# Sparse attention into a four-expert layer: weights asked for at other steps, a third buffer of v, first sums of x on VectorE, first attention steps in another order

## The chip, the cores and the metric

The kernel runs on one core of a Trainium2 chip. A core has TensorE (PE in the profile; its weight loads are shown apart as PEld), VectorE (DVE), ScalarE (ACT), GpSimd (POOL) and SyncE (SP), which here only issues transfers. The metric is device time in microseconds (us) for one execution, the median of several. The kernel before takes 1242.9 us (three executions: 1242.7, 1242.9 and 1249.59 us).

## What is computed

Attention for 4 batches, 8 heads, 768 positions and 64 channels a head. A query sees the first 8 keys and the 96 latest ones up to its own position, with a bias that falls with distance. Its result, reshaped to 3072 rows of 512, goes through four experts, each two matrix products with a relu between, mixed by given weights:

```python
scores = scale * q @ k.T + bias            # bias = -slope[head] * distance
scores = where(is_global | is_local, scores, -1e9)
x = softmax(scores) @ v                    # then reshaped to (3072, 512)
p = domain_probs / domain_probs.sum(-1)
out = sum over e of p[:, e] * (relu(x @ w1[e]) @ w2[e])
```

Everything is float32. w1 is (4, 512, 1024), w2 is (4, 1024, 512).

## The kernel before

**Batches and units.** The four batches of 768 rows go one after the other. A batch has 16 units (expert, quarter of its 1024 columns). `first(i)` is unit i's product with w1 and the relu, `second(i)` its product with w2, added to the output rows. The order is first(0), first(1), second(0), first(2), second(1) and so on. first yields 5 to 7 times (once for each of its products, which are Strassen-like combinations of blocks of x and of w1), second 6 times (once for each tile of 128 rows). Each yield is a step.

**Two halves of every number.** The big products multiply a rounded high half and a low half of each factor, so each product is three matmuls. x blocks and weights are therefore split first: `high` copies into the rounded type, `low` subtracts it from the source. Tiles w1s and w2s hold split weights, xB and xT split blocks of x and of sums of blocks (T1 to T4). A product of first is six matmuls of 128x384, and the second of these already needs a low half of the weights.

**Weights in batch 0.** `load_w1(i, wait, lead, hold, high)` works in steps: it waits `wait` steps, asks for the raw weights (one transfer into the only buffer raw1), waits `lead` steps, has GpSimd make four sums in `sums` (S1 to S4), waits `hold` steps, and then splits in four slices, a step each: high by ScalarE (for units 0 and 1 by GpSimd), low by GpSimd. `load_w2` does the same without sums. One such generator for unit i+2 starts with each first(i) and each second(i). w1s and w2s have two buffers each. After use they are written out to tiles named kept; batches 1 to 3 fetch them from there, so GpSimd splits weights in batch 0 alone.

**Attention.** Batches 1 to 3 have their attention woven into the units of the batch before (`attention`). Batch 0's attention has nothing to hide under and runs first, in `first_attention`: 12 steps d, each two tiles of 128 queries of one pair of heads, three steps a pair, pairs in the order 0, 2, 1, 3. `start` loads q and k of a pair, `start_v` its v (tiles first_v and first_vg, each with natv = 2 buffers), `turn_qk` transposes two tiles of q and k into early_q and early_k, `scores` multiplies them, `softmax` adds the bias nbias on VectorE and takes the exponential on ScalarE (pb), `turn` transposes the result (pT), `recip` inverts the sums (zr), `weigh_two` multiplies with v, `finish` writes x. Between the steps `forms_of` splits those blocks of x that are finished, and the first weights are loaded.

**What sets the order.** Every engine executes its own instructions in order, SyncE its transfers too: one that waits holds back those behind it. In the first attention and the first 7 steps of the units the order is that of the code (`Ordered.on`); after that a scheduler orders the work of each engine. Operations of these engines go through a helper and carry its line, L42, so instructions are told apart by the tiles they write and read.

## Time and profile before

| | |
|---|---|
| median of three executions | 1242.9 us |
| the profiled execution | 1247.98 us |
| its span, first to last instruction | 1245.7 us |
| PE busy in the span | 1191.1 us (96%) |
| DVE, ACT, POOL busy | 66%, 38%, 16% |
| mean granted TensorE clock | 0.976 of full speed |

Times in the views are microseconds from the start of the span, so the profiled execution's own time has 2.3 us around the span. In an instruction row stand the start, how long it (or the row of merged ones) lasted, engine, line, operation, the tile written and those read, shapes, and the count; in brackets the idle time of that engine just before, and what ended it. In a stretch row stand the busy time of each engine with its number of instructions, then PEclk, the granted TensorE clock (1.00 is 2.4 GHz, 0.50 is 1.2 GHz), the busy share of the transfer engines and GB/s. A wait row says who waited for whom: total us, how many times, the longest.

### The profile page before, as it was taken

What the parts mean: (1) busy time and instruction counts of PE and PEld (TensorE: products, weight loads), DVE (VectorE), ACT (ScalarE), POOL (GpSimd) and SP (SyncE); (2) the same over time, 40 slices, a digit from 0 to 9 for tenths busy, and PEclk for the clock granted to TensorE, in tenths of its full rate; (3) what the DMA queues carried; (4) which work ended last, traced back from release to release, by engine and by line L of the source; (5) the groups of instructions that cost most, each with busy time, mean ns of one, the idle gap of its engine ahead of it and who ended that gap; (6) DMA issues with size and microseconds to landing.
All of it is one profiled execution on the core that took longest, in us unless ns stands there. A gap on an engine that the chain in (4) does not pass through costs nothing.

```text
span 1245.7 us, 18214 instructions
## 1 busy us (share of the span) xinstructions
PE 1191.1 (96%) x6740; PEld 1063.7 (85%) x6740; DVE 826.2 (66%) x1771; ACT 478.1 (38%) x1234; POOL 202.3 (16%) x212
## 2 busy tenths in 40 slices
PE   7689798999999999999999999999999999999998
PEld 6578687878887898999898899989988899999997
DVE  6587455664757675766676877667666776666665
ACT  4444445554663254444443244444434221111110
POOL 3463533536365000000000100000000100000000
PEclk9789898998999999999999999999999999999999
DMA  7547659686598976766665775768474555555532
GB/s 127 113 168 204 203 160 304 194 265 209 178 329 304 276 224 203 227 191 224 210 194 188 249 227 191 213 188 251 154 230 159 201 212 186 188 189 186 186 131 87
DMA packets 146257, 252.97 MB, mean 203 GB/s; under 512 B 108273, under 2 KB 116465, under 8 KB 129777
## 3 DMA queue, kind: packets, MB, share of 16 engines
q1 hardware_dynamic: 142560, 245.44, 62.3%
q10 hardware_dynamic: 3600, 6.29, 1.4%
q8 instruction: 55, 0.90, 0.3%
q14 instruction: 42, 0.34, 0.1%
HBM read 180.41 MB, written 52.43 MB: 187 GB/s over the span
## 4 chain that ended last, share of the span: by engine, by line
PE 84%; POOL 4%; DVE 4%; DMA 3%; ACT 3%; issue 2%; SPq 0%; DVEq 0%; POOLq 0%; ACTq 0%
PE pm L42 73%; PE pt L42 6%; PE ps L42 4%; POOL w1s L42 2%; POOL sums L42 1%; DMA kept<-w1s 1%; POOL w2s L42 1%; DMA k<-in_k_dram 1%; ACT pb L42 1%; DMA qd<-st_q 1%; DMA raw<-in_moe_w_dram 0%; DVE pm L42 0%; DVE h L42 0%; DVE acc L42 0%; ACT xT L42 0%
## 5 line engine op out<-in xcount | busy, mean ns | idle before, releaser
L42 PE MATMUL pm<-w2s,h 128*128 128x512 f32 x2304 | 551.7, 394 | 3.6 <-DVE h L42 3.6
L42 PEld LDWEIGHTS pm<-w2s,h 128*128 128x128 f32 x2304 | 427.6, 188 | 92.9 <-DVE h L42 5.4
L42 DVE SCALAR_TENSOR_TENSOR acc<-pm,prob,acc 128x512 f32<-128x512 f32 x360 | 268.3, 749 | 158.2 <-PE pm L42 156.4
L42 PE MATMUL pm<-xT,w1s 128*128 128x384 f32 x1536 | 308.7, 347 | 6.6 <-POOL w1s L42 4.0
L42 PEld LDWEIGHTS pm<-xT,w1s 128*128 128x128 f32 x1536 | 276.9, 195 | 11.6 <-POOL w1s L42 6.5
L42 PE MATMUL pm<-xB,w1s 128*128 128x384 f32 x1152 | 231.2, 341 | 15.0 <-POOL w1s L42 13.9
L42 PEld LDWEIGHTS pm<-xB,w1s 128*128 128x128 f32 x1152 | 201.9, 189 | 20.9 <-POOL w1s L42 15.2
L42 ACT ACTIVATE h<-pm 128x384 fp32r<-128x384 f32 x256 | 124.8, 491 | 174.7 <-DVE pm L42 172.2
L42 DVE SCALAR_TENSOR_TENSOR h<-pm,h 128x384 fp32r<-128x384 f32 x256 | 140.8, 552 | 17.7 <-ACT h L42 13.0
L42 ACT ACTIVATE pb<-pb,nmax 128x256 f32<-128x256 f32 (+1 forms) x192 | 92.8, 485 | 100.6 <-DVE nmax L42 99.8
L42 ACT COPY p<-pm 128x384 f32<-128x384 f32 x64 | 30.5, 477 | 193.6 <-PE pm L42 184.3
L42 POOL TENSOR_TENSOR xT<-x,xT 128x768 fp32r<-128x768 f32 x3 | 5.5, 1837 | 569.1 <-ACT xT L42 569.1
L42 DVE TENSOR_TENSOR u<-pm,p 128x384 f32<-128x384 f32 x64 | 35.6, 557 | 84.4 <-PE pm L42 64.6
L42 ACT ACTIVATE pb<-pb,zsum 128x256 f32<-128x256 f32 (+1 forms) x144 | 63.3, 484 | 30.3 <-DVE zsum L42 30.2
L42 DVE TENSOR_TENSOR pm<-pm,vv 128x384 f32<-128x384 f32 x128 | 71.5, 559 | 2.0 <-PE pm L42 1.8
L42 POOL TENSOR_TENSOR w2s<-raw,w2s 128x512 fp32r<-128x512 f32 x32 | 42.0, 1333 | 160.1 <-ACT w2s L42 143.6
L42 DVE CUSTOM_DVE_ANT_0 pb<-ps,nbias 128x256 f32<-128x256 f32 (+1 forms) x144 | 52.5, 396 | 12.9 <-PE pt L42 11.1
L42 ACT COPY pT<-pt 128x512 f32<-128x512 f32 (+1 forms) x72 | 39.5, 550 | 55.0 <-PE pt L42 54.8
L42 PE MATMUL pt<-ident,pb 128*128 128x128 f32 x352 | 55.6, 282 | 0.0
L42 DVE TENSOR_TENSOR u<-pm,u 128x384 f32<-128x384 f32 x64 | 35.6, 557 | 28.1 <-PE pm L42 27.6
L42 DVE TENSOR_TENSOR vv<-pm,u 128x384 f32<-128x384 f32 x63 | 35.1, 557 | 27.2 <-PE pm L42 26.7
L42 PEld LDWEIGHTS pt<-ident,pb 128*128 128x128 f32 x352 | 43.2, 145 | 7.3 <-issue 4.5
(102 smaller groups left out, 905.0 us busy)
## 6 DMA issues: line engine op xcount, KB each, us to landing
w1s<-kept SPq DMA_DIRECT2D x48, 1792.0 KB, 7.5
w2s<-kept SPq DMA_DIRECT2D x48, 1024.0 KB, 4.9
kept<-w1s SPq DMA_DIRECT2D x16, 1792.0 KB, 8.6
qd<-st_q SPq DMA_DIRECT2D x96, 192.0 KB, 3.9
raw<-in_moe_w_dram SPq DMA_DIRECT2D x32, 512.0 KB, 6.0
kept<-w2s SPq DMA_DIRECT2D x16, 1024.0 KB, 8.4
out_dram<-acc ACTq DMA_DIRECT2D x24, 256.0 KB, 3.6
q<-in_q_dram SPq DMA_DIRECT2D x24, 192.0 KB, 6.5
```

The lines of the kernel that those rows point to most:

```text
L42: ins = fn(*args, **kwargs)
```

## The change

Six edits; none changes what is computed.

- The pool natv has three buffers of first_v and of first_vg. v of the later pairs is asked for one step after q and k of the same pair.
- In first_attention step 0 is written out ahead of the loop: its softmax comes before the scores of step 1, and the two early tiles of k of step 0 are copied from PSUM by ScalarE.
- w1 of unit 0 is asked for one step sooner, ahead of the second pair's v; w1 of unit 1 one step sooner; w2 of unit 0 eight steps later.
- T1 of the first block of x is subtracted by VectorE instead of GpSimd, and T3 is made at d = 8 and not at d = 9.
- w1 of unit 2 is asked for after 1 step instead of 6, ahead of w2 of unit 1, and split 5 steps sooner; w2 of unit 1 waits 6 steps instead of 12 before its split.
- For every later unit of batch 0, w1 is asked for after 4 steps instead of 9.

```diff
-            ve.tensor_copy(kT[:, ts[0] : ts[1] + 1, :P], tp[:, 2 * P :].rearrange("p (t c) -> p t c", c=P))
+            (ac.copy if d == 0 else ve.tensor_copy)(
+                kT[:, ts[0] : ts[1] + 1, :P], tp[:, 2 * P :].rearrange("p (t c) -> p t c", c=P)
+            )
...
-        start_v(ORDER[0])
         turn_qk(0)
         scores(0)
+        start_v(ORDER[0])
+        start(ORDER[1], slice(0, NQT))
+        softmax(steps[0])
+        next(bias)
         turn_qk(1)
-        yield
-        start(ORDER[1], slice(0, NQT))
+        scores(1)
+        softmax(steps[1])
+        turn_qk(2)
+        yield
         start_v(ORDER[1])
-        for d in range(last + 3):
+        for d in range(1, last + 3):
...
             if d % 3 == 1 and d // 3 + 2 < NPAIR:
                 start(ORDER[d // 3 + 2], slice(0, NQT))
+            if d % 3 == 2 and d // 3 + 2 < NPAIR:
                 start_v(ORDER[d // 3 + 2])
...
-            dict(setup=1, kd=2, qd=2, nat=2, natv=2, pb=6, pT=4, rT=2, small=6, sums=2), {},
+            dict(setup=1, kd=2, qd=2, nat=2, natv=3, pb=6, pT=4, rT=2, small=6, sums=2), {},
...
-            d = n - 1
-            if d == 1:
+            if d == 0:
                 chores.append(load_w1(0, 0, 1, 1, po.tensor_copy))
-            if d == 2:
-                chores.append(load_w2(0, 5, po.tensor_copy))
-            if d == 7:
+            if d == 6:
                 chores.append(load_w1(1, 0, 1, 0, po.tensor_copy))
+            if d == 10:
+                chores.append(load_w2(0, 2, po.tensor_copy))
             if d == 5:
-                forms_of(0, ("B11", "T1"), ac.copy, po, po, A)
+                forms_of(0, ("B11", "T1"), ac.copy, po, ve, A)
             if d == 8:
-                forms_of(0, ("B21", "B22"), ac.copy, po, po, A)
+                forms_of(0, ("B21", "B22", "T3"), ac.copy, po, ve, A)
             if d == 9:
-                forms_of(0, ("T3", "T2", "T4"), ac.copy, po, ve, A)
+                forms_of(0, ("T2", "T4"), ac.copy, po, ve, A)
...
-                chores += [load_w2(1, 12), load_w1(2, 6, 3)]
+                chores += [load_w1(2, 1, 4, 1), load_w2(1, 6)]
             else:
-                chores.append(load_w1(i + 2, 9) if fn is first else load_w2(i + 2))
+                chores.append(load_w1(i + 2, 4) if fn is first else load_w2(i + 2))
```

How the instructions stand in the built program, at three places. Behind a row stand the semaphores it waits for: DMAHW ones belong to earlier transfers, PE_49 to TensorE, Pool_49 to GpSimd, DVE_49 to VectorE.

SyncE in the first attention. Before, from the third pair's q and k to the first weights (raw_314 is w1 of unit 0, raw_380 w2 of unit 0):

```order
L42 DMA first_q<-in_q_dram 128x6x64 [waits DMAHW6_49,PE_49]
L42 DMA first_q<-in_q_dram 128x6x64 [waits DMAHW7_49]
L42 DMA first_k<-in_k_dram 128x6x64 [waits DMAHW0_49,PE_49]
L42 DMA first_k<-in_k_dram 128x6x64 [waits DMAHW1_49]
L42 DMA first_v<-in_v_dram 128x12x64 [waits DMAHW2_49,PE_49]
L42 DMA first_vg<-in_v_dram 96x12x64 [waits DMAHW3_49]
L42 DMA first_vg<-in_v_dram 32x6x64 [waits DMAHW4_49]
L42 DMA first_vg<-in_v_dram 32x6x64 [waits DMAHW5_49]
L42 DMA raw_314<-in_moe_w_dram 128x4x256 [waits DMAHW6_49]
L42 DMA raw_380<-in_moe_w_dram 128x2x512 [waits DMAHW7_49]
```

Now, SyncE from the second pair's k on (raw_248 is w1 of unit 0):

```order
L42 DMA first_k<-in_k_dram 128x6x64 [waits DMAHW0_49]
L42 DMA first_k<-in_k_dram 128x6x64 [waits DMAHW1_49]
L42 DMA raw_248<-in_moe_w_dram 128x4x256 [waits DMAHW2_49]
L42 DMA first_v<-in_v_dram 128x12x64 [waits DMAHW3_49]
L42 DMA first_vg<-in_v_dram 96x12x64 [waits DMAHW4_49]
L42 DMA first_vg<-in_v_dram 32x6x64 [waits DMAHW5_49]
L42 DMA first_vg<-in_v_dram 32x6x64 [waits DMAHW6_49]
L42 DMA first_q<-in_q_dram 128x6x64 [waits DMAHW7_49,PE_49]
L42 DMA first_q<-in_q_dram 128x6x64 [waits DMAHW0_49]
L42 DMA first_k<-in_k_dram 128x6x64 [waits DMAHW1_49,PE_49]
L42 DMA first_k<-in_k_dram 128x6x64 [waits DMAHW2_49]
L42 DMA first_v<-in_v_dram 128x12x64 [waits DMAHW3_49]
```

w1 of unit 0 stood behind the third pair's v, which waited for TensorE; it now stands ahead of the second pair's v, and the third v waits for no product.

GpSimd in batch 0, the weights of unit 3. Before (raw_1293 is w2 of unit 2, raw_1345 w1 of unit 3):

```order
L42 TENSOR_TENSOR w2s<-raw_1293,w2s 128x512 x2
L42 TENSOR_TENSOR sums<-raw_1345 128x256 x2
L42 TENSOR_TENSOR sums<-sums,raw_1345 128x256
L42 TENSOR_TENSOR w1s<-raw_1345,w1s 128x512
L42 TENSOR_TENSOR sums<-raw_1345,sums 128x256
L42 TENSOR_TENSOR w1s<-raw_1345,w1s 128x256
L42 TENSOR_TENSOR w1s<-sums,w1s 128x512 x2
```

Now, the same weights on GpSimd (raw_1272 is w1 of unit 3, raw_1306 w2 of unit 2):

```order
L42 TENSOR_TENSOR sums<-raw_1272 128x256 x2
L42 TENSOR_TENSOR sums<-sums,raw_1272 128x256
L42 TENSOR_TENSOR sums<-raw_1272,sums 128x256
L42 TENSOR_TENSOR w1s<-raw_1272,w1s 128x512
L42 TENSOR_TENSOR w1s<-raw_1272,w1s 128x256
L42 TENSOR_TENSOR w1s<-sums,w1s 128x512
L42 TENSOR_TENSOR w2s<-raw_1306,w2s 128x512
L42 TENSOR_TENSOR w1s<-sums,w1s 128x512
L42 TENSOR_TENSOR w2s<-raw_1306,w2s 128x512
```

w2 came first and held the sums back, since its low half waits for ScalarE's copy; now all four sums and three of the four w1 slices stand ahead of w2's last half.

SyncE in batch 0, where v of the third pair of batch 1's attention is loaded. Before (raw_1915 is w2 of unit 5, raw_1954 w1 of unit 6):

```order
L42 DMA qd<-st_q 64x768 [waits DMAHW1_49]
L42 DMA qd<-st_q 64x768 [waits DMAHW2_49]
L42 DMA vg<-in_v_dram 96x12x64 [waits DMAHW3_49,PE_49]
L42 DMA v<-in_v_dram 128x12x64 [waits DMAHW4_49,PE_49]
L42 DMA vg<-in_v_dram 32x6x64 [waits DMAHW5_49]
L42 DMA vg<-in_v_dram 32x6x64 [waits DMAHW6_49]
L42 DMA raw_1915<-in_moe_w_dram 128x2x512 [waits DMAHW7_49,Pool_49]
L42 DMA raw_1954<-in_moe_w_dram 128x4x256 [waits DMAHW0_49,Pool_49]
L42 DMA kept_1_1_2000<-w1s 128x3584 [waits DMAHW1_49,Pool_49]
```

Now, the same place of SyncE (raw_1854 is w1 of unit 6, raw_1917 w2 of unit 5):

```order
L42 DMA raw_1854<-in_moe_w_dram 128x4x256 [waits DMAHW6_49,Pool_49]
L42 DMA qd<-st_q 64x768 [waits DMAHW7_49,DVE_49]
L42 DMA qd<-st_q 64x768 [waits DMAHW0_49]
L42 DMA qd<-st_q 64x768 [waits DMAHW1_49]
L42 DMA qd<-st_q 64x768 [waits DMAHW2_49]
L42 DMA kept_3_2_1906<-w2s 128x2048 [waits DMAHW3_49]
L42 DMA v<-in_v_dram 128x12x64 [waits DMAHW4_49,PE_49]
L42 DMA vg<-in_v_dram 96x12x64 [waits DMAHW5_49]
L42 DMA vg<-in_v_dram 32x6x64 [waits DMAHW6_49]
L42 DMA vg<-in_v_dram 32x6x64 [waits DMAHW7_49]
L42 DMA raw_1917<-in_moe_w_dram 128x2x512 [waits DMAHW0_49,Pool_49]
```

w1 of unit 6 stood behind the v that waits for TensorE, and now stands ahead of it; w2 of unit 5 is still behind.

## Rows read from the trace of the kernel before

**Rows 1.** The page's first part: busy time of each engine, its share of the span, its instructions.

```profile
PE 1191.1 (96%) x6740; PEld 1063.7 (85%) x6740; DVE 826.2 (66%) x1771; ACT 478.1 (38%) x1234; POOL 202.3 (16%) x212
```

**Rows 2.** Stretches of the whole core: the stall in the first attention, batch 0's units, and batch 1's units up to 675 us.

```profile
38.00:49.60 11.60, 0.00 (x0) 0.00 (x0) 0.47 (x2) 2.80 (x11) 9.96 (x13) 0.67 0.34 66
...
89.30:395.60 306.30, 283.63 (x1542) 251.43 (x1542) 187.20 (x414) 157.06 (x391) 143.68 (x144) 0.94 0.73 237
395.60:675.00 279.40, 278.17 (x1582) 250.69 (x1584) 191.41 (x415) 113.33 (x301) 2.98 (x2) 0.99 0.70 218
```

**Rows 3.** The chain of work that ended last, in order of time: two of its pieces ahead of 49.6 us (start, us, what).

```profile
33.00 5.62 DMA raw<-in_moe_w_dram
...
45.57 0.96 POOL T L42
```

**Rows 4.** SyncE's transfers in order of time (start and length of the issue, not of the transfer).

```profile
10.46 1.58 SPq L42 DMA_DIRECT2D first_k<-in_k_dram  x2
...
17.89 1.69 SPq L42 DMA_DIRECT2D first_k<-in_k_dram  x2
30.03 0.37 SPq L42 DMA_DIRECT2D first_v<-in_v_dram  x1
```

**Rows 5.** GpSimd's instructions in order of time in the first attention.

```profile
11.18 7.41 POOL L42 TENSOR_SCALAR nbias<-dist 128x384 bf16<-128x384 f32 x6 [7.30 <-DVE dist L42]
38.70 0.72 POOL L42 TENSOR_TENSOR sums<-raw 128x256 f32<-128x256 f32 x1 [20.11 <-DMA raw<-in_moe_w_dram]
...
42.22 1.26 POOL L42 TENSOR_TENSOR w1s<-raw,w1s 128x512 fp32r<-128x512 f32 x1
```

**Rows 6.** Who waited for whom, ScalarE between 30 and 60 us.

```profile
ACT xT L42 <- POOL T L42: 11.7, 1, 11.7
```

**Rows 7.** VectorE's first bias addition (CUSTOM) of the steps d = 4, 5, 7, 8 and 9 of the first attention, in order of time.

```profile
26.27 0.42 DVE L42 CUSTOM_DVE_ANT_0 pb<-pm,nbias 128x256 f32<-128x256 f32 x1
...
30.00 0.42 DVE L42 CUSTOM_DVE_ANT_0 pb<-pm,nbias 128x256 f32<-128x256 f32 x1
...
50.01 0.41 DVE L42 CUSTOM_DVE_ANT_0 pb<-pm,nbias 128x256 f32<-128x256 f32 x1
...
55.03 0.42 DVE L42 CUSTOM_DVE_ANT_0 pb<-pm,nbias 128x256 f32<-128x256 f32 x1
...
59.67 0.28 DVE L42 CUSTOM_DVE_ANT_0 pb<-pm,nbias 128x128 f32<-128x128 f32 x1
```

**Rows 8.** Groups of VectorE's instructions by form from 0 to 38 us, where GpSimd is mostly idle: busy us, mean ns of one, idle before.

```profile
L42 DVE COPY early_k<-early_k 128x64 f32<-128x64 f32 x8 | 1.6, 204 | 0.1
...
L42 DVE TENSOR_SCALAR zr<-z 128x4 f32<-128x4 f32 x6 | 1.0, 159 | 0.0
```

**Rows 9.** The same groups from 49 to 90 us, where GpSimd is busy.

```profile
L42 DVE TENSOR_SCALAR zr<-z 128x4 f32<-128x4 f32 x6 | 2.9, 482 | 0.0
L42 DVE COPY early_k<-early_k 128x64 f32<-128x64 f32 x4 | 1.9, 483 | 0.0
L42 DVE TENSOR_TENSOR T<-x 128x384 f32<-128x384 f32 x3 | 1.9, 637 | 0.0
```

**Rows 10.** VectorE at the start, in order of time: the copies of early_k from PSUM for tiles 2, 3 and for tiles 4, 5 of the first pair.

```profile
9.52 0.42 DVE L42 COPY early_k<-ps 128x256 f32<-128x256 f32 x1 [1.80 <-ACT early_q L42]
...
13.69 0.42 DVE L42 COPY early_k<-ps 128x256 f32<-128x256 f32 x1 [1.08 <-ACT early_q L42]
```

**Rows 11.** Who waited for whom, TensorE between 90 and 400 us.

```profile
PE pm L42 <- POOL w1s L42: 17.9, 11, 4.2
PE pm L42 <- DVE h L42: 3.3, 3, 2.6
```

**Rows 12.** Stretches of batch 0 that hold those waits, five of them.

```profile
124.80:138.00 13.20, 8.37 (x33) 7.47 (x33) 2.74 (x9) 5.76 (x18) 8.48 (x10) 0.74 0.84 257
...
152.00:162.00 10.00, 7.18 (x33) 6.43 (x35) 1.28 (x3) 4.09 (x11) 5.84 (x7) 0.66 0.66 240
...
200.00:210.00 10.00, 6.34 (x22) 6.20 (x23) 1.09 (x3) 3.67 (x10) 6.68 (x8) 0.66 1.02 314
...
264.00:271.00 7.00, 4.69 (x17) 4.00 (x17) 1.47 (x8) 5.27 (x17) 4.43 (x4) 0.76 0.89 246
...
283.00:295.00 12.00, 8.99 (x34) 8.05 (x34) 3.37 (x9) 3.72 (x10) 8.13 (x9) 0.72 0.55 199
```

**Rows 13.** In order of time, the weights of unit 4 and the product that waits for them: relu of unit 3 and the split of w1 on ScalarE, the split of w2 and the first slice of w1 on GpSimd, the product on TensorE.

```profile
139.04 0.49 ACT L42 ACTIVATE h<-pm 128x384 fp32r<-128x384 f32 x1 [2.95 <-DVE pm L42]
...
148.17 2.54 POOL L42 TENSOR_TENSOR w2s<-raw,w2s 128x512 fp32r<-128x512 f32 x2 [14.89 <-ACT w2s L42]
...
148.93 0.91 ACT L42 CAST w1s<-raw 128x512 fp32r<-128x512 f32 x2
...
152.74 1.25 POOL L42 TENSOR_TENSOR w1s<-raw,w1s 128x512 fp32r<-128x512 f32 x1
...
154.05 1.51 PE L42 MATMUL pm<-xB,w1s 128*128 128x384 f32 x5 [2.71 <-POOL w1s L42]
```

**Rows 14.** SyncE's transfers in order of time: v of the third pair and the two raw weights behind it.

```profile
186.48 0.55 SPq L42 DMA_DIRECT2D v<-in_v_dram  x1
...
189.21 0.90 SPq L42 DMA_DIRECT2D raw<-in_moe_w_dram  x2
```

**Rows 15.** The transfers by issuing group: KB each, median us from issue to landing.

```profile
raw<-in_moe_w_dram SPq DMA_DIRECT2D x32, 512.0 KB, 6.0
```

More of the change, by code (lines that the diff above doesn't have):

```diff
@@ L614, in first_attention @@
         start(ORDER[0], slice(2, NQT))
-        start_v(ORDER[0])
         turn_qk(0)
         scores(0)
+        start_v(ORDER[0])
+        start(ORDER[1], slice(0, NQT))
+        softmax(steps[0])
+        next(bias)
         turn_qk(1)
+        scores(1)
+        softmax(steps[1])
+        turn_qk(2)
         yield
-        start(ORDER[1], slice(0, NQT))
         start_v(ORDER[1])
-        for d in range(last + 3):
+        for d in range(1, last + 3):
             if d + 1 <= last:
                 scores(d + 1)
-            for n in range(2):
-                if d <= last:
-                    softmax(steps[2 * d + n])
-                if d == 0 and n == 0:
-                    next(bias)
-            if d <= 2:
+            if d <= last:
+                softmax(steps[2 * d])
+                softmax(steps[2 * d + 1])
+            if d <= 3:
                 next(bias)
@@ L932, in attn_moe_kernel @@
             start_stack, "start",
-            dict(setup=1, kd=2, qd=2, nat=2, natv=2, pb=6, pT=4, rT=2, small=6, sums=2), {},
+            dict(setup=1, kd=2, qd=2, nat=2, natv=3, pb=6, pT=4, rT=2, small=6, sums=2), {},
         )
-        for n, _ in enumerate(first_attention(A, bank)):
-            d = n - 1
-            if d == 1:
+        for d, _ in enumerate(first_attention(A, bank)):
+            if d == 0:
                 chores.append(load_w1(0, 0, 1, 1, po.tensor_copy))
-            if d == 2:
-                chores.append(load_w2(0, 5, po.tensor_copy))
-            if d == 7:
+            if d == 6:
                 chores.append(load_w1(1, 0, 1, 0, po.tensor_copy))
+            if d == 10:
+                chores.append(load_w2(0, 2, po.tensor_copy))
             if d == 5:
-                forms_of(0, ("B11", "T1"), ac.copy, po, po, A)
+                forms_of(0, ("B11", "T1"), ac.copy, po, ve, A)
             if d == 8:
-                forms_of(0, ("B21", "B22"), ac.copy, po, po, A)
+                forms_of(0, ("B21", "B22", "T3"), ac.copy, po, ve, A)
             if d == 9:
-                forms_of(0, ("T3", "T2", "T4"), ac.copy, po, ve, A)
+                forms_of(0, ("T2", "T4"), ac.copy, po, ve, A)
             if d == 11:
```

## The prediction

> **What bounds the kernel now.** I read the page first: TensorE is busy 96% of the span [rows 1]. That is a mean over stages, so I cut the core's time into stretches and compared batch 0's units with batch 1's [rows 2]. Batch 1 executes 1582 matmuls in 279.4 us, 0.177 us each, at clock 0.99. Batch 0 executes 1542 in 306.3 us at 0.94; at batch 1's pace they would take 272 us. The reader is to see 34 us that batch 0 loses, and what differs between the two: GpSimd, busy 144 us in batch 0 against 3 us. Then the first attention: from 38.0 to 49.6 us TensorE executes nothing, VectorE two instructions, and GpSimd is busy 9.96 of 11.6 us [rows 2]. The rest, 850 us of the span from 395.6 us on, the change does not touch: its weights are fetched already split.
>
> **The stall in the first attention.** The chain of work passes there through the transfer of the first raw weights (33.00 us) and GpSimd's T, which ends at 46.5 us [rows 3]; ScalarE waits 11.7 us for that T [rows 6] and holds the exponentials back, and with them everything. T is late because it stands on GpSimd behind the sums and splits of unit 0's weights, and these wait 20.11 us for the raw weights [rows 5]. Those are late because SyncE, which had issued the third pair's k by 19.6 us, issues that pair's v only at 30.03 us [rows 4]: with two buffers it waits for the first pair's products with v.
>
> Now raw w1 of unit 0 stands right behind the second pair's k, issued by 12.0 us [rows 4]. With 6.0 us from issue to landing [rows 15] it is there at about 18 us instead of 38.7. GpSimd has the bias nbias first (7.41 us, of which a third now stands ahead of the sums) [rows 5], so it starts at about 18 us; the other two thirds and the work of the stall's stretch (4.9 + 9.96 us) [rows 2, 5] keep it to about 33 us. T is also no longer its work. So both causes go, one of which would do: **-11.6 us** [rows 2].
>
> What comes in their place:
> - T on VectorE, one instruction more in a step that VectorE bounds: at most 0.64 us, the mean under a busy GpSimd [rows 9]; I take **+0.6**.
> - GpSimd's splitting of unit 0's weights now lies under steps 2 to 6. Those were clean: step 4 to step 5 took 3.73 us [rows 7]. Two VectorE instructions of each step get longer where GpSimd is busy: zr from 159 to 482 ns, the small copy of early_k from 204 to 483 ns [rows 8, 9], 0.60 us a step, so **+3.0** for five steps. Lower bound 0, if they fall into VectorE's short waits; upper bound, each waits for one whole GpSimd subtraction of 1.26 us [rows 5], 2.5 us a step, 12.6 us. I take the means, since they are of the same two instructions under the same kind of work.
> - The start: VectorE stood idle 1.80 and 1.08 us ahead of two copies of early_k, for ScalarE [rows 10]. The first softmax now fills the first gap; early_k of step 0 moves to ScalarE. Between 0 and -2.9; the bias work still has to be done in between, so **-1.0**.
> - After the stall steps 7 and 8 took 5.02 and 4.64 us [rows 7] instead of 3.73, since the clock had fallen (0.67 of full over the stall's stretch) [rows 2]. Without the stall it should stay up, but GpSimd's work for unit 1 lies there: between 0 and -2.2, I take **-1.2**.
>
> T3 one step earlier is the same instruction elsewhere. w2 of unit 0, asked for at step 10, is needed only after first(1), and GpSimd is free by then; both cost nothing while first(0) and first(1) cover them. q, k and v of the later pairs keep several steps between issue and use. First attention: -11.6 + 0.6 + 3.0 - 1.0 - 1.2 = **-10.2**, bounds about -15 and 0.
>
> **The weights in batch 0.** TensorE waits 17.9 us in 11 waits for GpSimd's w1s [rows 11]. They fall into five stretches [rows 12], together 52.2 us with 33 + 33 + 22 + 17 + 34 = 139 matmuls. At 0.177 us these take 24.6 us, so the stretches lose 27.6 us: the waits, and some 10 us at a granted clock of 0.66 to 0.76, where it had fallen in the wait.
>
> Why it waits is seen in unit 4 [rows 13]. GpSimd's w2 starts at 148.17, its first w1 slice at 152.74, and the product that needs it had been waiting since 151.3. In the new order ScalarE's splits of that w1 stand right behind the first relu of unit 3, which is at 139.04, ten microseconds sooner than 148.93; then a slice is 1.25 us. In unit 3, where the copies stay behind the same exponentials, GpSimd has the sums done before and w2 behind: the first slice has two w2 and three sums less ahead of it (2.54 us and three times 0.72) [rows 5, 13], 4.7 us, more than the longest single wait, 4.2 us [rows 11]. At the stretch from 200 us the raw weights were issued at 189.21, behind a v that waited for TensorE until 186.48 [rows 14]; w1 now stands ahead of that v. So all five places are reached: **-27.6**.
>
> Not all of it will come. Unit 3's later slices stay tight, since w2's first half stands between them: about 1 us. In unit 4 raw1 is free only when unit 3's split is done, so the raw weights land some 6 us later [rows 15], a little after ScalarE reaches its copy; ScalarE then holds the relus behind it for 2 to 4 us, and four PSUM tiles let TensorE run on for about that long. I take **+3.5** for such places, between 0 and 10. Batch 0: **-24**, bounds -28 and -17. What is late next is the arithmetic itself: VectorE, 187 us busy of 282, as in batch 1 (191 of 279) [rows 2], and TensorE's waits for h of 3.3 us [rows 11], which I leave.
>
> **Sum.** -10.2 - 24 = -34. From the profiled execution, 1248.0 us, that gives 1214; it lies 5.1 us above the median, from which it gives 1209. I forecast **1210**.
>
> **Rivals.**
> - *GpSimd's work under VectorE's steps eats the first gain.* For it: the stall was the cover under which GpSimd could work without disturbing VectorE. At the upper bound the first attention gains 0 instead of 10: 1243 - 24 = **1219**. The Trainium skill (SBUF — State Buffer, Who interferes with whom) states such a rule: VectorE's copies and scalar operations, and its operations with two SBUF inputs such as T, share a port pair with GpSimd under an exclusive lock, and whichever comes second is blocked for the other's whole instruction. The rows agree that these instructions get longer [rows 8, 9], but by 0.3 us and not by a whole GpSimd instruction. By that rule at its worst the time is this rival's 1219. Chance 0.10.
> - *Batch 0's waits only change their name* (raw weights that land late, ScalarE's order): with half of the 24 us 1243 - 10 - 12 = 1221, with nearly none of it **1232**. Against it: w1s is what TensorE waits for, and its slices come sooner everywhere. Chance 0.12, half of it beyond 1230.
> - *Slower.* ScalarE now meets w1 sooner, and if it gets there before the raw weights have landed it waits with the relus and exponentials behind it. It decides from 34 / 14 = 2.4 us of TensorE time a unit, for the 14 units that split in batch 0; at the full 6.0 us from issue to landing [rows 15] it costs 84 us: 1243 - 34 + 84 = **1293**. Against it: raw1 is free, and the request out, long before the copy in all but two units. Chance 0.03.
> - *The first part does not do what it says*: raw w1 still lands late, or SyncE waits elsewhere, and the stall stays: 1243 - 24 = 1219. Chance 0.03.
>
> **How the numbers follow.** The likeliest case, both gains, has 0.72 and gives 1200 to 1220; the low end is 1243 - 15 - 28. The range reaches up to 1230, over rivals one and four and the better half of the second, and down to 1198 for a start that comes out better than I took it: that leaves about 0.15 out. Within 1% (about what a measurement of this kernel can tell from no change) is above 1230.5: half of the second rival, 0.06, and a little of the rest make 0.07; slower by over 1% is the third, 0.03; faster 0.90.
>
> **What would show it.** In the changed kernel's profile: no stretch after 20 us of the first attention in which TensorE executes nothing; the first raw weights issued near 12 us; GpSimd's sums at 18 us; zr and the small early_k between 0.16 and 0.5 us in steps 2 to 6; batch 0's units from about 79 us instead of 89.3. In batch 0: TensorE's waits for w1s under 5 us, a granted clock near 1.00, 280 us or a little more for its units. I am wrong if ScalarE shows waits for raw weights with h or p behind them on TensorE's chain, or if steps 2 to 6 take over 5 us each.

## The result, and the profile after

The changed kernel takes 1199.47 us in the median of four executions (1196.81 to 1203.07) against 1243.0 us before (four executions by then): a ratio of 0.9639, with the interval 0.9599 to 0.968. On a second chip it took 1200.41 us against 1246.75: 0.9627 (0.9611 to 0.9643). The forecast was 1210 us with a range of 1198 to 1230, so the time lies inside the range, near its low end, and the gain is some 45 us where the sum had 34. The profiled execution took 1196.81 us with a span of 1194.4. Ratios here and below leave out two disturbed executions, one each of e5 and e11.

The first part of the page of the changed kernel, which answers to [rows 1]:

```profile
PE 1171.8 (98%) x6740; PEld 1048.9 (88%) x6740; DVE 824.3 (69%) x1771; ACT 476.2 (40%) x1235; POOL 200.7 (17%) x211
```

The instructions are as many as they were, with one less on GpSimd and one more on ScalarE; the span is 51.3 us shorter, and the granted clock of the span 0.997 instead of 0.976. Stretches of the changed kernel: the place of the old stall, then batch 0's units up to about as many matmuls as before (1549 against 1542), to be laid beside [rows 2].

```profile
38.00:49.60 11.60, 11.15 (x124) 8.82 (x122) 11.46 (x45) 8.89 (x33) 8.68 (x11) 1.00 0.25 42
71.16:345.00 273.84, 270.61 (x1549) 242.02 (x1550) 188.24 (x417) 155.34 (x392) 145.66 (x150) 0.99 0.81 268
```

The reader is to see that TensorE works through the stall's place, with GpSimd nearly as busy as it was there (8.68 us against 9.96), and that batch 0 now runs at 273.84 / 1549 = 0.177 us a matmul, batch 1's pace. The transfers and GpSimd's start, in order of time, answer to [rows 4, 5]:

```profile
11.98 1.00 SPq L42 DMA_DIRECT2D raw<-in_moe_w_dram  x1
...
22.23 0.76 SPq L42 DMA_DIRECT2D first_v<-in_v_dram  x1
...
34.70 0.94 SPq L42 DMA_DIRECT2D raw<-in_moe_w_dram  x2
```

```profile
17.19 0.73 POOL L42 TENSOR_TENSOR sums<-raw 128x256 f32<-128x256 f32 x1 [5.10 <-DMA raw<-in_moe_w_dram]
```

The third pair's v goes out at 22.23 us instead of 30.03 right behind its k; unit 0's raw weights go out at 11.98, unit 1's (the first of the two in the last row) at 34.70. The steps d = 4, 5, 7, 8 and 9 in the changed kernel, VectorE's first bias addition of each, as in [rows 7]:

```profile
25.11 0.42 DVE L42 CUSTOM_DVE_ANT_0 pb<-pm,nbias 128x256 f32<-128x256 f32 x1
...
28.68 0.42 DVE L42 CUSTOM_DVE_ANT_0 pb<-pm,nbias 128x256 f32<-128x256 f32 x1
...
37.36 0.41 DVE L42 CUSTOM_DVE_ANT_0 pb<-pm,nbias 128x256 f32<-128x256 f32 x1
...
40.91 0.42 DVE L42 CUSTOM_DVE_ANT_0 pb<-pm,nbias 128x256 f32<-128x256 f32 x1
...
44.98 0.28 DVE L42 CUSTOM_DVE_ANT_0 pb<-pm,nbias 128x128 f32<-128x128 f32 x1
```

Step 7 begins 12.65 us earlier than before, step 9 14.69. Who waited for whom, TensorE in batch 0 of the changed kernel (71 to 350 us), as in [rows 11]:

```profile
PE pm L42 <- DVE h L42: 3.1, 3, 2.3
PE pm L42 <- POOL w1s L42: 0.5, 1, 0.5
```

The 17.9 us of waits for GpSimd's w1s are 0.5. No other wait has taken their place.

**The five places again.** Each of them in the kernel before, now with edges that fall on the same matmul in both kernels, and well clear of the slow part:

```profile
119.10:138.30 19.20, 14.37 (x63) 12.55 (x62) 7.16 (x23) 8.49 (x27) 9.64 (x10) 0.82 0.71 232
150.80:164.60 13.80, 10.31 (x55) 9.02 (x54) 2.66 (x6) 4.57 (x12) 7.04 (x8) 0.75 0.69 217
195.10:227.60 32.50, 27.66 (x134) 24.71 (x133) 15.59 (x39) 17.21 (x47) 19.52 (x20) 0.89 0.73 263
256.10:275.00 18.90, 16.34 (x80) 14.28 (x79) 10.88 (x31) 10.52 (x31) 7.29 (x8) 0.91 0.95 288
279.40:298.10 18.70, 15.69 (x72) 14.16 (x71) 7.43 (x19) 8.03 (x21) 9.68 (x10) 0.82 0.64 219
```

And the same matmuls (within two) in the changed kernel:

```profile
101.00:112.90 11.90, 11.41 (x61) 10.09 (x60) 7.12 (x23) 8.28 (x26) 8.07 (x8) 1.00 0.40 133
125.40:132.70 7.30, 7.30 (x56) 6.90 (x55) 2.64 (x6) 4.68 (x13) 5.23 (x8) 1.00 1.05 424
162.30:186.70 24.40, 24.40 (x134) 22.31 (x133) 15.37 (x37) 14.32 (x41) 12.98 (x13) 1.00 0.82 296
215.40:229.40 14.00, 14.00 (x78) 12.84 (x77) 10.00 (x25) 7.09 (x22) 2.14 (x3) 1.00 0.93 300
234.20:246.70 12.50, 12.50 (x72) 11.63 (x72) 7.62 (x20) 7.84 (x23) 6.74 (x8) 1.00 0.97 338
```

103.1 us have become 70.1: 33.0 us, with the clock at 1.00 in all five. The rows hold 404 and 401 matmuls, so some 0.5 us of that are the edges.

**One measure for all traces.** Every trace holds the 4992 matmuls that read w1s or w2s, in one fixed order, so each execution can be cut at the same matmul. The table gives the start of the first one (the end of the first attention, nearly) and the time from there to the 101st, the 601st, the 901st (the five places lie between the 101st and the 901st), the 1151st, the 1301st (batch 0's end) and the last. It is of the profiled execution of each kernel, in us; the experiments are told below.

| kernel | first | to 101 | to 601 | to 901 | to 1151 | to 1301 | to last |
|---|---|---|---|---|---|---|---|
| before | 77.2 | 24.7 | 142.6 | 85.8 | 58.0 | 36.4 | 815.1 |
| changed | 59.0 | 24.7 | 118.9 | 75.6 | 57.6 | 36.5 | 816.2 |
| e0, the changed kernel again | 62.6 | 24.6 | 119.0 | 75.6 | 57.6 | 36.8 | 816.0 |
| e1, first attention alone | 60.8 | 24.5 | 141.5 | 86.9 | 58.0 | 36.7 | 814.7 |
| e2, batch 0 alone | 81.2 | 24.3 | 118.9 | 75.6 | 57.7 | 34.2 | 818.3 |
| e3, two buffers of v | 63.6 | 30.9 | 118.9 | 75.7 | 57.6 | 36.5 | 814.9 |
| e4, T on GpSimd | 67.3 | 24.3 | 118.9 | 75.6 | 57.7 | 34.2 | 815.7 |
| e5, raw behind v, two buffers | 63.6 | 30.2 | 118.9 | 75.6 | 57.6 | 36.6 | 815.8 |
| e6, w2 of unit 0 early | 61.7 | 24.9 | 118.9 | 75.7 | 57.7 | 35.3 | 816.0 |
| e8, shorter lead alone | 60.8 | 24.5 | 119.1 | 75.4 | 57.6 | 33.9 | 815.2 |
| e9, raw late | 60.9 | 24.6 | 137.1 | 87.6 | 61.8 | 35.0 | 815.4 |
| e10, p first | 59.3 | 26.2 | 119.2 | 75.3 | 57.6 | 33.9 | 816.0 |
| e11, e8 again | 63.6 | 24.4 | 119.1 | 75.3 | 57.6 | 33.7 | 815.6 |
| e12, raw behind v, three buffers | 63.0 | 24.2 | 119.0 | 75.6 | 57.6 | 36.6 | 815.7 |

Between the two traces the first attention gains 77.2 - 59.0 = 18.2 us, batch 0 up to its 901st matmul 33.8, and nothing after that moves. The two together are 52, more than the 45 of the ratios, since the profiled execution of before is one of its longer ones and that of the changed kernel its shortest. The first column differs between single executions: the first attention of before takes 77.2 us and, in e2, 81.2, that of the changed kernel 59.0 to 63.6 (e0, e1, e8, e9 and e11 have the same one). By the traces its gain is 13.6 to 22.2 us.

### The profile page after: what moved, and what is told of

It reads as the page before. It is cut to its first block, busy times and chain, and to the rows that moved or that the text cites. A ratio compares the mean times of both kernels' runs of the same rounds, so it can differ in the third digit from the quotient of the medians.

```text
span 1194.4 us, 18187 instructions
## 1 busy us (share of the span) xinstructions
PE 1171.8 (98%) x6740; PEld 1048.9 (88%) x6740; DVE 824.3 (69%) x1771; ACT 476.2 (40%) x1235; POOL 200.7 (17%) x211
## 4 chain that ended last, share of the span: by engine, by line
PE 89%; DVE 5%; DMA 3%; ACT 1%; SPq 1%; issue 1%; POOL 0%; DVEq 0%; POOLq 0%
PE pm L42 80%; PE pt L42 6%; PE ps L42 3%; DMA qd<-st_q 1%; DVE pb L42 1%; DVE pT L42 1%; SPq L42 1%; DMA out_dram<-acc 1%; DVE early_k L42 0%; DMA q<-in_q_dram 0%; DVE zr L42 0%; DMA first_k<-in_k_dram 0%; DMA raw_n<-in_n_local_dram 0%; DVE T L42 0%; ACT xT L42 0%
## 5 line engine op out<-in xcount | busy, mean ns | idle before, releaser
L42 PE MATMUL pm<-xT,w1s 128*128 128x384 f32 x1536 | 297.9, 338 | 3.1 <-ACT p L42 2.1
L42 PEld LDWEIGHTS pm<-xT,w1s 128*128 128x128 f32 x1536 | 267.9, 189 | 5.5 <-ACT p L42 2.4
L42 PE MATMUL pm<-xB,w1s 128*128 128x384 f32 x1152 | 227.2, 339 | 0.0
L42 ACT ACTIVATE pb<-pb,zsum 128x256 f32<-128x256 f32 (+1 forms) x144 | 63.1, 484 | 18.0 <-DVE zsum L42 17.9
L42 PE MATMUL ps<-kd,qd 128*128 128x256 f32 x288 | 47.8, 283 | 0.6 <-DMA qd<-st_q 0.4
## 6 DMA issues: line engine op xcount, KB each, us to landing
kept<-w1s SPq DMA_DIRECT2D x16, 1792.0 KB, 10.2
```

Of the source, the lines that this page charges most:

```text
L42: ins = fn(*args, **kwargs)
```

## The experiments

The theory is that of the prediction: two separate gains, the stall in the first attention and GpSimd's late weights in batch 0.

**e1 and e2: each part alone.** e1 is the changed kernel with

```diff
-                chores += [load_w1(2, 1, 4, 1), load_w2(1, 6)]
+                chores += [load_w2(1, 12), load_w1(2, 6, 3)]
-                chores.append(load_w1(i + 2, 4) if fn is first else load_w2(i + 2))
+                chores.append(load_w1(i + 2, 9) if fn is first else load_w2(i + 2))
```

> The changed kernel with the old requests for batch 0's weights (load_w2(1, 12), load_w1(2, 6, 3), load_w1(i + 2, 9)), so only the part of the first attention is left. By the prediction's sum it gains 10.2 us against the kernel before, 1243 - 10 = 1233 us, and 24 us lie between it and the changed kernel. By the trace of the changed kernel, in which the first unit's run of products starts at 71.16 us instead of 89.29, it gains 18 us: 1225. Rival: part of those 18 us is handed back where batch 0 waits anyway for weights; then 1230 to 1238 though its products also start near 71 us. TensorE's waits for GpSimd's w1s are 15 to 20 us in each case.

e2 is the kernel before with the opposite edit.

> The kernel before with the new requests for batch 0's weights alone (load_w1(2, 1, 4, 1), load_w2(1, 6), load_w1(i + 2, 4)). By the prediction's sum it gains 24 us: 1219; by the five stretches in full 27.6: 1215. Rival: the gain in batch 0 needs the first part too, since the first units' weights come out of the stall; then under 15 us: 1228 or more. The start of the first unit's products stays at 89 us.

e1 took 1231.05 us against 1247.02: ratio 0.9876 (0.9839 to 0.9912), a gain of 15.5 us. e2 took 1211.42: 0.9717 (0.9692 to 0.9742), a gain of 35.3. In the table e1 has the early start (60.8) and every loss of batch 0 (TensorE waits 18.5 us for w1s), e2 the late start (81.2) and none of those losses. So the two gains are separate. It is the table that shows this and not the times: e1's interval reaches from 11.0 to 20.1 us, which leaves its rival open, but up to the 901st matmul e1 takes 252.9 us where before takes 253.1, so nothing is handed back there; and e2, with 218.8, has the whole gain of batch 0 without the first part. In the times the two add up to 50.8 us, 4 to 6 more than the changed kernel's 45.0 and 46.5, about what the intervals allow. Both are larger than the terms of the sum, 10.2 and 24.

**e4: T on GpSimd again.**

```diff
-                forms_of(0, ("B11", "T1"), ac.copy, po, ve, A)
+                forms_of(0, ("B11", "T1"), ac.copy, po, po, A)
```

> The changed kernel with T of unit 0's first blocks taken on GpSimd again; the raw weights are still asked for early. The prediction holds that either cause alone, once gone, ends the stall: then T stands about 1 us behind GpSimd's splits, no stretch near 38 us is empty on TensorE, and the time is that of the changed kernel within 2 us (1197 to 1202). Rival: T on GpSimd is the cause by itself, and the stall comes back with 5 to 12 us: 1204 to 1211.

1198.88 us, 0.9613 (0.9588 to 0.9638): the changed kernel's time within its interval of 3 us either way. A remainder of the stall is there, though, against the expectation: ScalarE's waits for GpSimd's T, which were 11.7 us in one [rows 6], are in e4

```profile
ACT xT L42 <- POOL T L42: 2.1, 1, 2.1
```

So with the raw weights early, four fifths of that wait are gone. T on VectorE is worth 3 to 4 us in the traces (from step 6 to the first unit 29.8 us in e4, 26.2 in the changed kernel, 26.5 in e0). The times do not show it; e4's trace gets 2.3 us of it back at batch 0's end, the place told of under e8.

**e3, e5 and e12: the early request and the third buffer.** e3 is the changed kernel with natv=2. e5 asks for unit 0's raw w1 at d = 1, behind the third pair's v, which is put back right behind its k, with natv=2; e12 is e5 with natv=3.

```diff
-            if d % 3 == 2 and d // 3 + 2 < NPAIR:
                 start_v(ORDER[d // 3 + 2])
...
-            if d == 0:
+            if d == 1:
                 chores.append(load_w1(0, 0, 1, 1, po.tensor_copy))
```

> The changed kernel with two buffers of v. The raw weights of unit 0 are still asked for before the third pair's v, so nothing that is needed soon stands behind the v that waits: the time stays that of the changed kernel within 1.5 us. Rival: SyncE's wait for the buffer, until the first pair's products with v near 30 us, holds unit 1's raw weights and the fourth pair's q and k back, and steps 9 to 11 or unit 1's first product wait: 3 to 8 us slower.

> The changed kernel with raw w1 of unit 0 asked for one step later, the third pair's v right behind its k as before, and two buffers of v: so the raw weights stand behind a v that waits, and land near 38 us again, while T stays on VectorE. If one cause alone, once gone, is enough: no stall at 38 us, and at most 3 us lost later, since GpSimd's splits of unit 0 run to about 50 us: 1199 to 1203. Rival: GpSimd's late splits hold the lower parts of x's blocks and unit 0's first product, and the run of products starts 5 to 12 us later than 71.16: 1204 to 1211.

> The changed kernel with raw w1 of unit 0 asked for one step later and behind the third pair's v, as in e5, but with three buffers of v. With e3 and e5 it fills the square of the two edits. If the third buffer is what counts, since SyncE then waits for no v: raw w1 of unit 0 is issued near 25 us and that of unit 1 near 35, and the time is the changed kernel's within 1.5 us (ratio to the kernel before 0.962 to 0.964). Rival: the early request of unit 0 counts by itself, and GpSimd's sums some 10 us later push its splits of unit 1 into the first products, TensorE waits for GpSimd's xB as in e3: 3 to 6 us slower.

| | unit 0's raw asked early | behind v |
|---|---|---|
| three buffers | 0.9627 (0.9611 to 0.9643), e0 | 0.9623 (0.9588 to 0.9659), e12 |
| two buffers | 0.9669 (0.9653 to 0.9685), e3 | 0.9700 (0.9652 to 0.9747), e5 |

The third buffer is what counts, by 5.1 us on one chip (e0 against e3; e12 against e5 points the same way, with a wide interval); the early request by itself, which the prediction spoke of, changes nothing that can be seen in the time. My expectations for e3 and e5 were wrong, their rivals came. The old stall is gone in all three: from step 6 to step 7 they take 4.44 us (e3), 3.51 (e5) and 4.15 (e12). In e5, where unit 0's raw weights go out at 32.41 us and two buffers are left, it is T's move that does it. What is late in e3 is unit 1's weights. SyncE's transfers in e3:

```profile
11.72 1.02 SPq L42 DMA_DIRECT2D raw<-in_moe_w_dram  x1
...
32.94 0.37 SPq L42 DMA_DIRECT2D first_v<-in_v_dram  x1
...
48.07 0.94 SPq L42 DMA_DIRECT2D raw<-in_moe_w_dram  x2
```

Unit 0's raw weights are early, but the third pair's v waits for its buffer until 32.94 us, the fourth pair's until 44.86; each holds back everything behind it, and unit 1's raw weights go out at 48.07 instead of 34.70. (In e12 they go out at 38.11, in e5 at 46.55.) GpSimd is late by as much at the end, and TensorE waits for it there once, in a stretch in which nothing else runs (e3, TensorE's wait, then the stretch):

```profile
PE pm L42 <- POOL xB L42: 4.8, 1, 4.8
```

```profile
65.00:70.00 5.00, 0.41 (x1) 0.41 (x2) 0.00 (x0) 0.00 (x0) 4.84 (x6) 0.97 0.00 0
```

In the table this is the 30.9 us to the 101st matmul, against 24.6; e5 has 30.2, and a wait for GpSimd's xB of 4.3 us.

**GpSimd's work under VectorE's steps.** In steps 2 to 6 e1 and e5 differ on GpSimd, which splits weights and computes nbias there in e1 and is empty in e5, and in the order of the transfers; VectorE's instructions are the same. Groups of VectorE from 16 to 37 us, e1 first, then e5:

```profile
L42 DVE TENSOR_SCALAR zr<-z 128x4 f32<-128x4 f32 x5 | 2.3, 460 | 0.0
L42 DVE COPY early_k<-early_k 128x64 f32<-128x64 f32 x5 | 1.1, 217 | 0.1
```

```profile
L42 DVE COPY early_k<-early_k 128x64 f32<-128x64 f32 x6 | 1.1, 187 | 0.1
...
L42 DVE TENSOR_SCALAR zr<-z 128x4 f32<-128x4 f32 x6 | 1.0, 159 | 0.0
```

And the first bias addition of steps 2 and 7, e1 first, then e5:

```profile
18.73 0.41 DVE L42 CUSTOM_DVE_ANT_0 pb<-pm,nbias 128x256 f32<-128x256 f32 x1
...
38.98 0.41 DVE L42 CUSTOM_DVE_ANT_0 pb<-pm,nbias 128x256 f32<-128x256 f32 x1
```

```profile
18.37 0.42 DVE L42 CUSTOM_DVE_ANT_0 pb<-pm,nbias 128x256 f32<-128x256 f32 x1
...
37.03 0.42 DVE L42 CUSTOM_DVE_ANT_0 pb<-pm,nbias 128x256 f32<-128x256 f32 x1
```

Five steps take 20.25 us with GpSimd at work and 18.66 without: 1.6 us. (The changed kernel's own first profile has 20.25 too; e12, with GpSimd busy half of that time, lies between.) The groups stop at 37 us and miss one copy of the last step: counted from 18.73 to 38.98 us in e1 and from 18.37 to 37.03 in e5, zr goes from 159 to 443 ns and the small copy of early_k from 186 to 350, 1.4 and 0.8 us in five steps. Most of the latter is one copy of 0.94 us. It stands in the changed kernel too, with GpSimd's subtraction beside it:

```profile
36.51 0.94 DVE L42 COPY early_k<-early_k 128x64 f32<-128x64 f32 x1
```

```profile
36.12 1.27 POOL L42 TENSOR_TENSOR w1s<-sums,w1s 128x512 fp32r<-128x512 f32 x1
```

The copy ends at 37.45, GpSimd's instruction at 37.39, and so it is with the other long zr and copies beside GpSimd's sums, casts and subtractions (zr at 23.69 us took 0.88 and ended at 24.57, GpSimd's subtraction at 24.55): VectorE waited for the rest of the instruction that GpSimd was in. Not every overlap costs it: at 25.01 us, with GpSimd in an nbias instruction from 24.51 to 25.68, the same copy took 0.18.

**e6: w2 of unit 0 where it was.**

```diff
+            if d == 2:
+                chores.append(load_w2(0, 5, po.tensor_copy))
-            if d == 6:
+            if d == 7:
                 chores.append(load_w1(1, 0, 1, 0, po.tensor_copy))
-            if d == 10:
-                chores.append(load_w2(0, 2, po.tensor_copy))
```

> The changed kernel with unit 0's w2 asked for at step 2 and unit 1's w1 at step 7, as before. Steps 7 to 11 gained 4.4 us in the first traces, of which the prediction gave 1.2 to the clock. If the place of GpSimd's work on w2 and on unit 1's w1 made the difference, steps 9 and 10 take 1 to 2 us longer than the changed kernel's and the time is 1.5 to 4 us more; if the clock and T3's place alone made it, the time is the same within 1 us.

1200.05 us, 0.9638 (0.9614 to 0.9661): the same. The move of w2, which the sum had at nothing, is worth nothing that can be seen in the time. In the trace steps 9 and 10 take 9.04 us, where the changed kernel's two traces have 8.48, T4 alone 1.51 instead of 0.56.

**e8 and e11: the shorter lead of the later units alone.** The changed kernel with the old pair of requests at the first unit:

```diff
-                chores += [load_w1(2, 1, 4, 1), load_w2(1, 6)]
+                chores += [load_w2(1, 12), load_w1(2, 6, 3)]
```

> The changed kernel with the old first pair of requests (load_w2(1, 12), load_w1(2, 6, 3)), but the new shorter lead of all later ones (load_w1(i + 2, 4)). In the trace of before no product is late until the run of unit 1's second products (some 175 products of batch 0 done), and then five stretches lose 33 us. If the shorter lead makes it, the time stays that of the changed kernel within 2 us; if the first pair is needed, since the raw buffer is taken over from unit to unit, the first stretch of 7 us or more of the five come back: 1206 to 1230.

> e8's kernel again, as the measure of e10 on the same chip, and to see whether its 1195.6 us, 4.8 below the changed kernel on one chip, comes back. The traces put 1.8 us of it at the first 25 us (granted clock 0.66 and 0.50 in the changed kernel's execution, 0.66 and 1.00 in e8's) and 2.4 us at the end of batch 0 (clock 0.56 against 1.00), both places whose instructions hardly differ. If these are the clock's accidents, the ratio to the kernel before comes back between the two, 0.960 to 0.963; if the old first pair is better by itself, it stays at 0.9596 or under.

e8: 0.9596 (0.9575 to 0.9617); e11: 0.9589 (0.9571 to 0.9608). All of batch 0's gain is that of one number, 9 to 4; the new first pair of requests does not add to it. (By which of the orders that follow from it, GpSimd's or SyncE's, the five places gain was not tried one by one.) This version is the fastest of the study, executions of 1193.9 to 1199.1 us, 4.8 us under the changed kernel on the same chip (1195.59 against 1200.41). The table shows 0.3 to 0.6 us of it up to the 901st matmul and 2.6 to 3.1 at batch 0's end, where e8's and e11's traces have the clock at 1.00 and the changed kernel's falls. Stretches there, e8 first, then the changed kernel:

```profile
340.00:343.00 3.00, 1.98 (x12) 1.66 (x10) 3.00 (x7) 3.00 (x7) 3.00 (x2) 1.00 0.95 395
343.00:346.00 3.00, 2.52 (x11) 2.13 (x12) 2.57 (x5) 1.53 (x4) 3.00 (x3) 1.00 0.98 313
```

```profile
341.00:344.00 3.00, 1.03 (x4) 0.86 (x5) 3.00 (x5) 2.32 (x5) 3.00 (x3) 1.00 0.79 273
344.00:347.00 3.00, 3.00 (x9) 2.29 (x8) 2.33 (x4) 0.38 (x1) 3.00 (x2) 0.53 0.91 382
```

The changed kernel's TensorE also stands idle longer there before its clock falls: 1.97 us in its first row, 1.02 and 0.48 in e8's two. e6 idles as long as the changed kernel (1.81 us from 344 to 347 us), keeps the clock and takes 35.3 us: so some 1.2 us are the clock. e2 and e4, with the new pair, idle still less than e8 (1.03 us) and take 34.2, so the old pair is not needed for that. By what I had written down for e11 (0.9596 or under) the old pair would be better by itself; the traces do not show by what, and I leave it open. That the version is no slower is measured.

**e9: the request late, the splits not moved in the code.**

```diff
-                chores.append(load_w1(i + 2, 4) if fn is first else load_w2(i + 2))
+                chores.append(load_w1(i + 2, 8, 1) if fn is first else load_w2(i + 2))
```

> The changed kernel with batch 0's raw w1 asked for four steps of a unit later, and the sums and splits where they are now in the order (load_w1(i + 2, 8, 1)). A step is about 281.8 / (16 x 13) = 1.35 us, so ScalarE meets its copy three steps, 4.1 us, behind the request, and the landing takes 6.0: it waits some 2 us a unit with the relus behind it, and GpSimd's sums come some 4.6 us later than now. The prediction's slower rival said that ScalarE's wait would be paid by TensorE beyond 2.4 us a unit; by it TensorE waits for h, and 14 units cost 0 to 28 us. Rival: ScalarE's wait is covered, and what is paid is GpSimd's lateness, as before the change: TensorE waits for w1s, 5 to 25 us. If neither is paid, there are 4 us of slack and the time is the changed kernel's.

1229.43 us, 0.9851 (0.9829 to 0.9874): some 28 us of the gain are gone, and by the table most of them where the kernel before lost them (18.1 us up to the 601st matmul, 12.0 up to the 901st, against e0) and 4.2 up to the 1151st. TensorE waits 14.9 us for w1s and 5.8 for h in batch 0. ScalarE waits for no raw weights at all; its waits for GpSimd's sums are in e9, in the kernel before and in the changed kernel, over batch 0's units:

```profile
ACT w1s L42 <- POOL sums L42: 35.2, 22, 3.4
```

```profile
ACT w1s L42 <- POOL sums L42: 35.6, 22, 3.4
```

```profile
ACT w1s L42 <- POOL sums L42: 9.8, 12, 1.3
```

So e9 is the kernel before again, though its code issues sums and splits at the changed kernel's steps. GpSimd in order of time shows what happened, unit 3's weights in e9, then in the changed kernel:

```profile
107.04 2.55 POOL L42 TENSOR_TENSOR w2s<-raw,w2s 128x512 fp32r<-128x512 f32 x2 [14.80 <-ACT w2s L42]
109.53 1.42 POOL L42 TENSOR_TENSOR sums<-raw 128x256 f32<-128x256 f32 x2
```

```profile
98.50 1.45 POOL L42 TENSOR_TENSOR sums<-raw 128x256 f32<-128x256 f32 x2 [7.96 <-DMA raw<-in_moe_w_dram]
...
105.30 2.02 POOL L42 TENSOR_TENSOR w1s<-raw,w1s 128x512 fp32r<-128x512 f32 x2 [3.83 <-ACT w1s L42]
107.27 1.30 POOL L42 TENSOR_TENSOR w1s<-sums,w1s 128x512 fp32r<-128x512 f32 x1
108.51 1.29 POOL L42 TENSOR_TENSOR w2s<-raw,w2s 128x512 fp32r<-128x512 f32 x1
```

With the request late, the scheduler puts w2 first and the sums behind it, as in the kernel before; GpSimd then stands idle for 14.80 us, at last for ScalarE's copy of w2, while w1's sums, which need no other engine, wait behind. At this unit the order alone is the cause: SyncE issued both raw weights by 95.9 us, at the same place as in the changed kernel (there from 92.51, and e9 runs 1.7 us behind it), and the trace has 5.9 to 7.0 us from issue to landing, so they were there by 102.0, and the sums start at 109.53. For later units, whose requests do go out later, lateness of the landing and the order were not told apart: no run had a late request with the new order.

**e10: the last wait of the first attention.** e8's kernel with unit 1's p copied first:

```diff
-                forms_of(1, ("B22", "T3", "T2", "T4"), ac.copy, ve, ve, A)
                 begun[2] = up1.tile([P, HALF], F32, name="p1")
                 ac.copy(begun[2], product(1, "A11", "B11")[:, :HALF])
+                forms_of(1, ("B22", "T3", "T2", "T4"), ac.copy, ve, ve, A)
```

> e8's kernel (shorter lead alone) with one thing more: at the end of the first attention the copy of unit 1's first product p is issued ahead of the forms of x's second blocks, not behind them. In the changed kernel TensorE waits 2.1 us for that copy at 69.30 us, and the granted clock falls to 0.66 from 70 to 75 us behind it. If that wait is the only thing late there, it gains 2 us of the wait and 1 to 2 us of the clock: 1192 to 1194 us. Rival: T2's and T4's lower parts of the second blocks on VectorE are late by nearly as much, and the wait takes the name of VectorE's xT or h: the time is e8's within 1 us.

1197.44 us, 0.9606 (0.9588 to 0.9624), against e11's 0.9589 on the same chip: no gain. TensorE's wait for p (2.1 us) is gone, and one for h of 2.8 us stands in its place, as the rival had it:

```profile
PE pm L42 <- DVE h L42: 2.8, 1, 2.8
```

**e0: the changed kernel again**, on the chip of e3, e6 and e8.

> The changed kernel once more, on the same chip as the three that follow, as their measure. By its first runs 1197 to 1203 us, median 1199.5. What differs between its executions should be the granted clock of TensorE in single stretches: if the first 25 us of the attention run at half clock in this profile, steps 2 to 4 take some 2 us longer than in the first profile of the changed kernel.

1200.41 us, and the first 25 us did run at a lower clock in its profile; steps 2 to 4 take 12.88 us instead of 11.57, 1.3 longer where I had expected 2. The rows are in the last section.

## Why the prediction was right, and where its sizes were off

**The stall** (-11.6) is right: from step 6 to step 7 the traces go from 16.20 us to 4.52, -11.7. "Both causes go, one of which would do" is right for T (e5) and nearly so for the request (e4). What the sum had no term for is the third buffer, 5 us of the gain: unit 0's request is early by its place alone (e3), but with two buffers unit 1's raw weights stay late, and then TensorE waits for GpSimd at the end of the first attention. The prediction read [rows 4] only for the first raw weights behind the waiting v and did not follow the queue on to unit 1's.

**T on VectorE** (+0.6): 0.55 us, right; it stands in step 5, ahead of step 6's first addition.

**GpSimd under VectorE's steps** (+3.0): the term was mis-sized, 1.6 by e1 and e5. zr was nearly as forecast (443 ns, forecast 482), the small copy of early_k shorter (350 ns, forecast 483): 2.2 us in five steps, of which 1.6 show in the time. Its sign, 0.16 to 0.5 us each, holds for the means but not for single ones (0.88 and 0.94 us in the changed kernel). The rival of 1219 us, with VectorE waiting for whole GpSimd instructions, is out. By the rule in the Trainium skill (SBUF — State Buffer, Who interferes with whom) whichever of the two engines issues first has the shared ports for its whole instruction, and the other is blocked. The trace agrees in the long instructions, which end with GpSimd's; but VectorE comes in the middle of one, or in a pause, so the mean is 0.28 us more for zr and 0.16 for the copy beside instructions of 0.6 to 1.3 us. The whole of one is the worst case (zr 1.25 us, once, in e12) and not the price.

**The start** (-1.0): -2.0 in the changed kernel's first trace (step 2 at 17.11 us instead of 19.12), -0.4 in e1's, whose clock was lower there: right within what single executions differ by.

**Steps 7 and 8** (-1.2): mis-sized. They take 40.91 - 37.36 = 3.55 and 4.07 us instead of 5.02 and 4.64, -2.0, nearly the whole of the bound of -2.2, though T3's 0.55 us now lie in step 8; GpSimd's work for unit 1 cost next to nothing there. Steps 9 and 10 gave another 2.4 (from 59.67 to 70.53 us before, 44.98 to 53.46 now), which the sum did not have. Most of it can be read: T2 and T4 take 0.55 us each where they took 0.97 beside GpSimd's sums, 0.8 together, and T3's 0.55 are made a step earlier. e6 puts 0.6 of it at the place of w2 and unit 1's w1. The rest is not settled.

**Batch 0** (-27.6 + 3.5): mis-sized, -33.8. Within the exact edges of [rows 12], 52.2 us in all, the same matmuls, found by their number in the trace, take 23.3 us where the forecast gave them 24.6: 28.9 lost. The larger part is the edges: they were drawn around the waits, and what is lost just outside them, where the clock has not come back or TensorE already runs short, is 33.0 - 28.9 = 4.1 us more. And the 3.5 us for places that stay tight did not come: ScalarE does wait for raw weights, once for 3.1 us and once for 0.9, but TensorE's waits for h stay at 3.1 us, so it was covered. The prediction had the better measure on the page before: batch 0 at batch 1's pace, 34 us less [rows 2]. It came out to the microsecond in the traces.

**The slower rival** did not come: those two waits are all that ScalarE waits for raw weights. e9 shows that the room is small all the same. Four steps later at the request bring back nearly all of the loss, through GpSimd's order and not through ScalarE's wait for the landing as the rival had it.

**In sum** -18 and -34 in the traces, where the prediction had -10 and -24; by e1 and e2, -15.5 and -35.3. Along the steps the 18.2 us of the first attention are 2.0 gained up to step 2, 1.0 lost in steps 2 to 5 (T among it), 11.7 gained in step 6, 2.0 in steps 7 and 8, 2.4 in 9 and 10, and 1.1 from step 11 to the first unit; the last two have no term in the sum. The best case of its own terms adds up to -16.1 (the prediction wrote about -15), and the trace lies beyond that. Both terms erred to the same side, because each took only what lay inside the stretch of the wait and too little of the low clock behind it, and because possible losses were taken at the middle of their bounds and turned out near the low end.

## What to carry to other kernels

A stage that has a sibling with the same arithmetic is measured best against the sibling's pace: it counts the low clock and the thin edges around a wait, which stretches cut around the waits leave out. On an in-order queue follow a waiting transfer to everything behind it, not only to the first thing that is late: here one more buffer, by which nothing waits, did more than a better place for one request. And where a scheduler sets the order, the step at which a transfer is asked for can decide the order of the work that uses it, even if that work's place in the code is untouched (e9).

## What the hardware showed that was not expected

The profiled executions of these kernels differ in two places almost alone. From the 101st to the 1151st matmul, all kernels with the lead of 4 agree within 0.3 us in the table, on several chips. The start and the end of batch 0 do not. The same instructions from 10 to 25 us ran in the changed kernel's first profile at

```profile
10.00:15.00 5.00, 3.38 (x25) 2.40 (x26) 3.44 (x18) 2.72 (x10) 2.01 (x2) 1.00 1.26 214
15.00:20.00 5.00, 3.88 (x39) 2.94 (x39) 4.66 (x17) 3.56 (x14) 2.73 (x4) 1.00 1.30 252
20.00:25.00 5.00, 4.71 (x56) 3.69 (x52) 4.66 (x18) 2.79 (x11) 4.77 (x6) 1.00 0.98 186
```

and in e0's, the same program, at

```profile
10.00:15.00 5.00, 3.63 (x20) 2.44 (x20) 3.07 (x17) 2.65 (x10) 1.76 (x2) 0.67 1.35 211
15.00:20.00 5.00, 4.00 (x22) 2.93 (x18) 3.37 (x13) 1.86 (x8) 2.45 (x4) 0.50 1.29 246
20.00:25.00 5.00, 4.72 (x42) 3.53 (x40) 3.82 (x13) 2.25 (x9) 4.77 (x6) 0.80 1.30 216
```

In the ten microseconds ahead of this TensorE was busy 6.79 us in the one and 6.41 in the other; it then ran at full speed in the one and fell to half (1.2 GHz) in the other, whose first unit begins at 62.6 us instead of 59.0. That busy time does not tell which way it goes: in e4 it was 7.01 us, and the clock from 10 to 15 us was 0.52. At batch 0's end the time to the 1301st matmul lies between 33.7 and 36.8 us, in part by the clock, in part by how long TensorE idles there (e8). Where one program has two profiles, the first place has nearly all of the difference: 3.6 of 3.8 us between the changed kernel's and e0's, 2.8 of 3.1 between e8's and e11's. A single profile's difference of a few microseconds at these places says nothing of an edit.
